# Attention with a gated feed-forward: the P.V sums and scores of the last two turns, and two output tiles

## The chip, the cores and the metric

The kernel runs on one core of a Trainium2 chip. The metric is the device time of one execution in microseconds; a kernel's time is the median over its runs. The engines are TensorE (PE, with its weight loads as PEld), VectorE (DVE), ScalarE (ACT), GpSimd (POOL) and SyncE (SP, which here only issues DMAs). Each works through its own instructions in program order and waits on semaphores of the others.

## The reference

With S = 2048 rows, D = 512, H = 32 heads of 16 and F = 1792:

```python
def _A_ref(x, wqkv, wo):
    qkv = ((x @ wqkv).reshape(B, S, 3, H, Dh)).transpose(2, 0, 3, 1, 4)
    q, k, v = qkv[0], qkv[1], qkv[2]
    scores = jnp.einsum("bhqd,bhkd->bhqk", q, k) * Dh ** -0.5
    o = jnp.einsum("bhqk,bhkd->bhqd", softmax(scores), v)
    return o.transpose(0, 2, 1, 3).reshape(B, S, D) @ wo

def _B_ref(x, w1, b1, w2, b2):
    h = jnp.einsum("bsd,df->bsf", x, w1) + b1
    r = jnp.where(h > 0, h, 0)
    return jnp.einsum("bsf,fd->bsd", r * r, w2) + b2

xn = _layernorm(A_x)
out = A_x + _A_ref(xn, A_wqkv, A_wo) * silu(_B_ref(xn, B_w1, B_b1, B_w2, B_b2))
```

## The kernel before

**Tiling.** After a first part (layer norm, transposes, queries, keys and values, written to DRAM) the attention runs in 512 steps `(qd, qc, kb)`: eight groups of four heads, four chunks of 512 queries, sixteen blocks of 128 keys. A step has two pairs of scores (`p` = 0, 1; two heads each, a tile of 128 keys x 2 x 512 queries), their exponentials in a tile `P`, and four matmuls of P.V (`values`, L572), each of which writes 32 of the 128 partitions of one PSUM bank: 16 value sums of a head and, from a column of ones, its row sum.

**Turns.** Eight steps make a turn, so there are 64 turns, and two of them make a chunk of queries for four heads. A turn `n` issues the 16 pairs of scores of the *next* eight steps and then the P.V matmuls of its own eight, 64 matmul records. The steps end at 511, so the last turn has 14 pairs. Between the scores TensorE does another product half by half (`lin`, L344, bank pair `spare`): the feed-forward, and in the last eight turns the projection with `wo`. The order within a turn is written out by hand as a string: `S` is a pair of scores into a tile "S", `0`, `1` and `B` are halves of a pair that go "aside", `L` is one step of the other product, `/` swaps the product's halves. Python code records the instructions in that order; no scheduler moves them (`manual_schedule`).

**PSUM.** The eight banks are: two rotating tiles "S" of two banks each (`BUFS["S"] = 2`), `spare` with two, and `sides[0]` ("acc") and `sides[1]` ("lin") with one each. `sides[0]` is also the bank in which P.V is summed. A pair in "S" is read by one exp of ScalarE straight out of PSUM (`exps`, L300, `P<-S`). An aside pair goes as two halves through `sides[0]` and `sides[1]`; VectorE copies each to the `P` tile (`aside`, L319), and ScalarE takes the exp in place (`P<-P`). Nine pairs are `direct` first, five (`pairs[9:14]`) are asides, and the last two are direct again but are held back in `later`: their exps are issued behind those of the asides. In the last turn those last two pairs don't exist.

**Sums.** `finish` copies the bank at the end of an even turn to `ou` (L583) and adds it to the bank at the end of the odd one (L586). The last turn leaves it to the end of the kernel (L880), where two adds of 128 x 256 do it.

**The end.** The last chunk of 512 rows needs the sums of the last turn. Behind its P.V stand: `ou` (L880), four matmuls with the identity that turn the row sums (L885), reciprocal, 16 matmuls that spread it (L892), the product (L904), a split in two parts (L905, L907), the projection (L704), the gate (L920), and the add of the input (L924, L927) or an accumulating store (L922). The third chunk's part of the same heads (`rest(i, dst)`, three matmuls of L704, and `end_rest(i, src)`) is spread among this: `rest(0)` stands in the last turn ahead of P.V and writes into a tile `two` of tag "S"; `rest(2)`, `rest(3)` and `rest(1)` come in the tail. `end_rest` gates a tile of 128 x 512 and adds it to the rows in DRAM with an accumulating DMA of POOL. Those rows were stored before from `base[2, i]`, which stays in SBUF.

Of the kernel before, what the change touches and what calls it, by code (L numbers as in the profile page):

```python
# [28 lines left out]
OP = mybir.AluOpType  # L29
# [45 lines left out]
def fast_path(tc, sb, ps, env):  # L75
# [4 lines left out]
    x, wqkv, wo, w1, b1, w2, b2, out = (  # L80
        env[n] for n in ("x", "wqkv", "wo", "w1", "b1", "w2", "b2", "out"))
    mm = nc.tensor.matmul
    dve, act, pool, sp = nc.vector, nc.scalar, nc.gpsimd, nc.sync
# [3 lines left out]
    def t(shape, dt, tag):  # L87

        cnt[0] += 1
        p = ps if tag in ("S", "lin", "acc") else sb  # L90
        if tag in BUFS:
            turn[tag] = turn.get(tag, -1) + 1
            n = turn[tag] % BUFS[tag]
            tag = f"{tag}{places[n] if tag == 'S' else n}"
        return p.tile(shape, dt, tag=tag, name=f"{tag}_{cnt[0]}")
# [194 lines left out]
    ptile = {}  # L290

    def score(i, p, hp, dst):
        qd, qc, kb = steps[i]
        k, q = ka[qd, kb // 8], qa[qd, qc]
        r = slice(64 * hp, 64 * hp + 64)
        mm(dst, k[r, p, 128 * (kb % 8):128 * (kb % 8) + 128], q[r, p], start=True, stop=True)  # L296

    def exps(i, p, src):
        if src is not None:
            act.activation(ptile[i, p], src, AF.Exp, scale=SCALE)  # L300

    def place(i, p):
        ptile[i, p] = t([128, 2, 512], FT, f"P{2 * ((i - 1) % 8) + p}")

    def scores(i, p):

        if i < len(steps):
            sc = t([128, 2, 512], FT, "S")
            place(i, p)
            for hp in range(2):  # L310
                score(i, p, hp, sc[:, hp])
            return sc

    def aside(i, p, hp):

        if hp == 0:
            place(i, p)
        score(i, p, hp, sides[hp])
        dve.tensor_copy(ptile[i, p][:, hp], sides[hp])  # L319

    gated, complete, gates = {}, set(), set()

# [35 lines left out]
    def lin(*halves):  # L358
        done = False
        if pair[0]:  # L360
            for half in halves:
                j = half ^ swapped[0]
                done |= pair[0][j].issue(half, lin_banks[j])
        return done

    def swap():
        if pair[0]:
            while lin(0, 1):
                pass
            f = pool.memset(note[:, notes[0]:notes[0] + 1], 0.0)  # L370
            notes[0] += 1
            for block in pair[0]:
                tc.add_manual_dep(f.ins, block.last, SYNC, reason="the products so far")
            swapped[0], fence[0] = 1, f.ins.name
# [53 lines left out]
    def second(c, g, i):  # L428
        ms = [m for m in range(len(PAIRS)) if PAIRS[m][0] == g]
        h, w = [hid[m] for m in ms], [wf[2, m] for m in ms]  # L430

        def evict():
            if g == 0:
                y[c, i] = t([128, 2, 512], FT, f"y{i}")
            old = b2b.unsqueeze(1).broadcast_to([128, 2, 512]) if g == 0 else y[c, i]
            dve.tensor_tensor(y[c, i], spare, old, op=OP.add)
            if g == 3:
                complete.add((c, i))

        return [Block(lambda p, k, j=j: h[k // 2][p][:, k % 2, 128 * j:128 * j + 128],  # L440
                      lambda p, k: w[k // 2][p][:, k % 2], range(2 * len(ms)), evict)
                for j in (2 * i, 2 * i + 1)]
# [8 lines left out]
    for c in ORDER:  # L451
        for m in range(len(PAIRS)):
            fill.append([lambda m=m: first(m)])
            if m in (1, 2, 4, 6):
                makes = [lambda c=c, g=m // 2, i=i: second(c, g, i) for i in range(2)]
# [113 lines left out]
    def values(i):  # L569
        qd, qc, kb = steps[i]  # L570
        for j in (1, 2, 3, 0) if i % 2 else (0, 1, 2, 3):
            mm(sides[0][32 * j:32 * j + 32], vq[qd][:, kb, 17 * j:17 * j + 32], ptile[i, j // 2][:, j % 2],  # L572
               start=kb % 8 == 0, stop=kb % 8 == 7)

    part = [None]

    def finish(n):

        if n == TURNS - 1:
            return  # L580
        ou = t([128, 512], FT, "ou")
        if n % 2 == 0:
            dve.tensor_copy(ou, sides[0])  # L583
            part[0] = ou
            return
        dve.tensor_tensor(ou, sides[0], part[0], op=OP.add)  # L586
        qd, qc, _ = steps[8 * n]
        sp.dma_start(zdram[qd][qc], ou[16::32])
        for j in range(4):
            sp.dma_start(udram[qd // 2][qc][0, qd % 2, :, j], ou[32 * j:32 * j + 16])  # L590
        events.setdefault(2 * n + 2, []).insert(0, (load_sums, (qd, qc)))
        events.setdefault(2 * n + 3, []).insert(0, (rowsums, (qd, qc)))
# [39 lines left out]
    wos, gsb, pend, onorm, base = [None], {}, {}, {}, {}  # L632
# [94 lines left out]
    TURNS, LAST = len(steps) // 8, 8 * (NQ - 1)  # L727
# [42 lines left out]
    def happen(time):  # L770
        for fn, a in events.pop(int(2 * time), ()):
            fn(*a)


    n = turn["S"]
# [5 lines left out]
    sides = [t([128, 512], FT, "acc"), t([128, 512], FT, "lin")]  # L781
# [6 lines left out]
    def end_rest(i, src):  # L788

        o = t([128, 512], FT, f"wf2{'hl'[i // 2]}{i % 2}")  # L790
        dve.scalar_tensor_tensor(o, src, 0.5, gsb[2, i // 2][:, i % 2], op0=OP.mult, op1=OP.mult)
        pool.dma_start(out[1024 + 128 * i:1152 + 128 * i], o, accum_op=OP.add)

    seen = t([1, 16], FT, "seen")

    def see(i):

        last = ptile[i, 1][:1, 1, 511:]
        act.copy(seen[:, :1], last)
        dve.tensor_tensor(seen[:, 8:9], last, sides[1][:1, :1], op=OP.max)  # L800
# [4 lines left out]
    ORDINARY = "SLLSBLLLSLL0SL1LSLL/SBLLSLL0SL1LSLL0L1SLS"  # L805
    TWO_PAIRS = "SLLLLBLLS/SL0LL1SLLSSEBLLLSLLLS/BLLSLL0LS1S"

    FIRST = "SLLSLLBLSLL0SL1LSLL/SBLLSLL0SL1LSLL0L1SLS"
    for n in range(TURNS):
        i = 8 * n  # L810
        happen(n)
        makes = fill[n][:]
        pair[0] = makes.pop(0)()
        if n:
            see(i - 1)
        pairs = [(k, p) for k in range(i + 1, i + 9) for p in range(2)]
        direct, asides = pairs[:9] + pairs[14:], pairs[9:14]
        later, aside_at = [], [0, 0]
        for row in TWO_PAIRS if makes else ORDINARY if n else FIRST:
            if row == "S":  # L820
                k, p = direct.pop(0)
                sc = scores(k, p)
                if k == i + 8:
                    later.append((k, p, sc))
                else:
                    exps(k, p, sc)
            elif row == "L":
                lin(0, 1)
            elif row in "01B":
                for hp in (0, 1) if row == "B" else (int(row),):  # L830
                    aside(*asides[aside_at[hp]], hp)
                    aside_at[hp] += 1
                if row != "B":
                    lin(1 - int(row))
            elif row == "/":
                swap()
                if n == TURNS - 1:
                    make_on((2, 3))
            else:
                end_pair()  # L840
                pair[0] = makes.pop(0)()
        for j, (k, p) in enumerate(asides):
            exps(k, p, ptile[k, p])
            if j == 0:
                for fn, a in middle.pop(n, ()):
                    fn(*a)
        for a in later:
            exps(*a)
        if n == TURNS - 1:
            two = t([128, 2, 512], FT, "S")  # L850
            rest(0, two[:, 0])
        pieces_now = pieces_of[n] if n < len(pieces_of) else 0
        ahead = pieces_now > 0 and n % per in (0, 1, 3, 6, 7, 10, 11)
        while lin(0, 1):
            pass
        if ahead:
            split_piece()
        end_pair()
        if n == LAST - 1:
            gsb.update({(2, i): y[2, i] for i in range(2)})  # L860
        if n == TURNS - 1:
            end_rest(0, two[:, 0])
        happen(n + 0.5)
        for _ in range(pieces_now - ahead):
            split_piece()
        for j in range(8):
            values(i + j)
        finish(n)
    for time in sorted(events):
        happen(time / 2)  # L870


    ou = t([128, 512], FT, "P0")
# [3 lines left out]
    h, l = t([128, 512], FR, "wf1h0"), t([128, 512], FR, "wf1l0")  # L877
    half = [slice(0, 256), slice(256, 512)]
    for s in half:
        dve.tensor_tensor(ou[:, s], sides[0][:, s], part[0][:, s], op=OP.add)  # L880
    small = t([128, 2, 512], FT, "S")
    lins = [small[:, 1], t([128, 512], FT, "lin"), t([128, 512], FT, "acc"), two[:, 0]]
    rest(2, spare[:, 0])
# [6 lines left out]
    for i in range(4):  # L890
        for j in range(4):
            mm(small[32 * j:32 * j + 32, 0, cut[i]], r[:, 4 * i + j:4 * i + j + 1].broadcast_to([128, 32]), ident,  # L892
               start=True, stop=True)
# [18 lines left out]
    o = [t([128, 512], FT, f"P{2 + i}") for i in range(4)]  # L912
    for j in range(2):
        for todo in ((0, 0), (0, 1)), ((1, 0),):
            for i in (2 * j, 2 * j + 1):
                group(lins[i], lambda p: (h, l)[p][:, cut[i]], lambda p: wlast[0][:, p],
                      start=len(todo) == 2, stop=len(todo) == 1, todo=todo)
        for i in (2 * j, 2 * j + 1):
            rows = out[1536 + 128 * i:1664 + 128 * i]
# [121 lines left out]
```

## Time and profile before

| | |
|---|---|
| median of 3 runs | 1227.74 us (1227.72 to 1228.27) |
| profiled execution | 1226.96 us, span 1224.9 us, granted clock 0.997 |
| TensorE busy | 1211.4 us (99%) |
| ScalarE busy | 1011.6 us (83%) |
| VectorE busy | 810.9 us (66%) |
| POOL busy | 279.6 us (23%) |

A timeline row has its start and length in us, the engine, the line, operation and operands, the count, and in brackets how long the engine stood idle before and what ended that. A chain row has start, length, engine, tile, line and count. A group has the count, then the busy time, the mean of one in ns, and the idle time ahead. A window has its length, the busy time and count of PE, PEld, DVE, ACT and POOL, the granted clock, the DMAs' share and GB/s. "P<-S" is an operation that reads a tile "S" and writes a tile "P"; numbers of buffers are left out.

### The profile page before, as it was taken

What the parts mean: (1) busy time and instruction counts of PE and PEld (TensorE: products, weight loads), DVE (VectorE), ACT (ScalarE), POOL (GpSimd) and SP (SyncE); (2) the same over time, 40 slices, a digit from 0 to 9 for tenths busy, and PEclk for the clock granted to TensorE, in tenths of its full rate; (3) what the DMA queues carried; (4) which work ended last, traced back from release to release, by engine and by line L of the source; (5) the groups of instructions that cost most, each with busy time, mean ns of one, the idle gap of its engine ahead of it and who ended that gap; (6) DMA issues with size and microseconds to landing.
All of it is one profiled execution on the core that took longest, in us unless ns stands there. A gap on an engine that the chain in (4) does not pass through costs nothing.

```text
span 1224.9 us, 24017 instructions
## 1 busy us (share of the span) xinstructions
PE 1211.4 (99%) x9925; PEld 717.4 (59%) x9925; DVE 810.9 (66%) x1293; ACT 1011.6 (83%) x1172; POOL 279.6 (23%) x223
## 2 busy tenths in 40 slices
PE   9999999999999999999999999999999999999997
PEld 8888755555555555555555555555555555555554
DVE  4542277676767775757686666676765758777776
ACT  4222489999999999999998998899999999999993
POOL 5000032122221220404022222130230403322212
PEclk9999999999999999999999999999999999999998
DMA  8675823232161323223423214141422232365445
GB/s 318 247 269 191 268 76 110 70 96 62 51 198 49 98 69 101 79 78 112 150 63 112 62 54 126 34 171 45 135 79 79 76 99 79 113 203 168 133 152 138
DMA packets 103750, 147.30 MB, mean 120 GB/s; under 512 B 42826, under 2 KB 57176, under 8 KB 102100
## 3 DMA queue, kind: packets, MB, share of 16 engines
q1 hardware_dynamic: 100484, 136.28, 35.0%
q0 software_dynamic: 2720, 8.65, 2.5%
q8 instruction: 79, 1.29, 0.4%
q10 hardware_dynamic: 432, 0.79, 0.2%
q14 instruction: 35, 0.29, 0.1%
HBM read 99.68 MB, written 46.00 MB: 119 GB/s over the span
## 4 chain that ended last, share of the span: by engine, by line
PE 97%; ACT 2%; DVE 0%; issue 0%; POOL 0%; DVEq 0%; POOLq 0%; ACTq 0%
PE acc L572 37%; PE spare L344 28%; PE S L296 14%; PE S L112 10%; PE acc L296 4%; ACT P L300 2%; PE lin L296 2%; PE lin L474 1%; PE S L210 1%; PE acc L112 0%; PE lin L112 0%; PE S L704 0%; PE acc L704 0%; DVE P L920 0%; DVE P L927 0%
## 5 line engine op out<-in xcount | busy, mean ns | idle before, releaser
L300 ACT ACTIVATE P<-S 128x1024 f32<-128x1024 f32 x704 | 664.5, 1037 | 91.3 <-PE S L296 91.3
L572 PE MATMUL acc<-P,V 128*32 128x512 f32 x4096 | 452.7, 594 | 0.0
L319 DVE COPY P<-acc 128x512 f32<-128x512 f32 x320 | 221.4, 692 | 143.6 <-PE lin L296 72.0
L300 ACT ACTIVATE P<-P 128x1024 f32<-128x1024 f32 x320 | 313.0, 1086 | 0.0
L572 PEld LDWEIGHTS acc<-P,V 128*32 128x32 f32 x4096 | 126.5, 110 | 287.4 <-issue 268.1
L296 PE MATMUL S<-QA,KA 64*128 64x512 f32 x1408 | 291.2, 403 | 3.0 <-ACT P L300 3.0
L319 DVE COPY P<-lin 128x512 f32<-128x512 f32 x320 | 219.4, 686 | 1.1
L296 PEld LDWEIGHTS S<-QA,KA 64*128 64x128 f32 x1408 | 134.1, 184 | 113.5 <-issue 43.5
L105 POOL TENSOR_TENSOR wf1l<-wr,wf1h 128x1024 fp32r<-128x1024 f32 x28 | 68.5, 2447 | 291.1 <-ACT wf1h L99 111.6
L296 PE MATMUL lin<-QA,KA 64*128 64x512 f32 x320 | 126.0, 394 | 0.0
L296 PE MATMUL acc<-QA,KA 64*128 64x512 f32 x320 | 125.8, 393 | 0.0
L370 POOL MEMSET note<- 1x1 f32 x68 | 6.1, 89 | 395.3 <-PE spare L344 392.9
L344 PE MATMUL spare<-xl,wf1h 64*128 64x512 f32 x464 | 96.1, 391 | 0.0
L105 POOL TENSOR_TENSOR hl<-T,hh 128x1024 fp32r<-128x1024 f32 x28 | 80.0, 2858 | 52.9 <-DVE hh L101 51.0
L344 PE MATMUL spare<-xh,wf1l 64*128 64x512 f32 x480 | 91.6, 390 | 0.0
L344 PE MATMUL spare<-wf2l,hh 64*128 64x512 f32 x448 | 91.0, 390 | 0.0
L105 POOL TENSOR_TENSOR wf2l<-wr,wf2h 128x1024 fp32r<-128x1024 f32 x28 | 67.2, 2399 | 90.3 <-DVE wf2h L101 90.3
L586 DVE TENSOR_TENSOR ou<-acc,ou 128x512 f32<-128x512 f32 x31 | 21.5, 692 | 97.6 <-PE acc L572 87.8
L344 PE MATMUL spare<-wf2h,hl 64*128 64x512 f32 x448 | 83.5, 390 | 0.0
L344 PE MATMUL spare<-xh,wf1h 64*128 64x512 f32 x480 | 77.1, 392 | 0.0
L344 PE MATMUL spare<-wf2h,hh 64*128 64x512 f32 x448 | 71.8, 392 | 0.0
L583 DVE COPY ou<-acc 128x512 f32<-128x512 f32 x32 | 22.2, 692 | 70.9 <-PE acc L572 70.5
(239 smaller groups left out, 1332.0 us busy)
## 6 DMA issues: line engine op xcount, KB each, us to landing
wr<-in_B_w_dram SPq DMA_DIRECT2D x56, 512.0 KB
KA<-kd SPq DMA_DIRECT2D x64, 256.0 KB
QA<-qd SPq DMA_DIRECT2D x128, 128.0 KB
kd<-P SPq DMA_DIRECT2D x15, 512.0 KB
qd<-P SPq DMA_DIRECT2D x15, 512.0 KB
u<-ud SPq DMA_DIRECT2D x15, 512.0 KB
V<-vd SPq DMA_DIRECT2D x8, 664.0 KB
vd<-P SPq DMA_DIRECT2D x16, 280.0 KB
```

Source lines behind the costliest of these rows:

```text
L105: leng.tensor_tensor(lo, src, hi.bitcast(FT), op=OP.subtract)
L112: mm(dst, lhs(a, k), rhs(b, k), start=n == 0, stop=n == len(todo) - 1)
L210: nc.tensor.transpose(pt[:, k, 128 * j:128 * j + 128], xnorm[c, i][:, j, 128 * k:128 * k + 128], ident)
L296: mm(dst, k[r, p, 128 * (kb % 8):128 * (kb % 8) + 128], q[r, p], start=True, stop=True)
L300: act.activation(ptile[i, p], src, AF.Exp, scale=SCALE)
L319: dve.tensor_copy(ptile[i, p][:, hp], sides[hp])
L344: ins = mm(bank, self.lhs(a, k)[r], self.rhs(b, k)[r], start=n == 0 and self.at[other] == 0, stop=n == len(self.todo[half]) - 1 and self.a ...
L370: f = pool.memset(note[:, notes[0]:notes[0] + 1], 0.0)
L474: mm(idle[:, :128], ident, ident, start=True, stop=True)
L572: mm(sides[0][32 * j:32 * j + 32], vq[qd][:, kb, 17 * j:17 * j + 32], ptile[i, j // 2][:, j % 2], start=kb % 8 == 0, stop=kb % 8 == 7)
L583: dve.tensor_copy(ou, sides[0])
L586: dve.tensor_tensor(ou, sides[0], part[0], op=OP.add)
```

## The change

In the last two turns P.V adds up in one bank without a copy between: the first matmul of turn 63 doesn't clear it, and `finish` does nothing for both turns. So `sides[0]` can't take scores in the last turn. That turn has its own string, `FINAL`, with eleven direct pairs and three asides, whose halves both go through `sides[1]`, one after the other. The last two direct pairs (`waits`) are held back behind the asides' exps, as the last two are in the other turns. At the end ScalarE copies the sums to `ou` in two halves where VectorE added them. `end_rest` for tiles 0 and 2 adds the kept `base` tile on POOL and stores with a plain DMA of SP; tiles 1 and 3 go on accumulating.

```diff
-    def aside(i, p, hp):
+    def aside(i, p, hp, bank):
...
-        score(i, p, hp, sides[hp])
-        dve.tensor_copy(ptile[i, p][:, hp], sides[hp])
+        score(i, p, hp, sides[bank])
+        dve.tensor_copy(ptile[i, p][:, hp], sides[bank])
...
             mm(sides[0][32 * j:32 * j + 32], vq[qd][:, kb, 17 * j:17 * j + 32], ptile[i, j // 2][:, j % 2],
-               start=kb % 8 == 0, stop=kb % 8 == 7)
+               start=kb % 8 == 0 and i // 8 < TURNS - 1, stop=kb % 8 == 7 and i // 8 != TURNS - 2)
...
-        if n == TURNS - 1:
+        if n > TURNS - 3:
             return
...
-        pool.dma_start(out[1024 + 128 * i:1152 + 128 * i], o, accum_op=OP.add)
+        rows = out[1024 + 128 * i:1152 + 128 * i]
+        if i % 2:
+            pool.dma_start(rows, o, accum_op=OP.add)
+        else:
+            pool.tensor_tensor(o, o, base[2, i // 2][:, 0], op=OP.add)
+            sp.dma_start(rows, o)
...
+    FINAL = "S0LSLLL1SLLS0LLSLL1S/LSLL0LSLLSL1LSLLLS"
...
         direct, asides = pairs[:9] + pairs[14:], pairs[9:14]
+        if n == TURNS - 1:
+            direct, asides = pairs[:9] + pairs[12:14], pairs[9:12]
+        waits = direct[-2:]
...
-        for row in TWO_PAIRS if makes else ORDINARY if n else FIRST:
+        for row in TWO_PAIRS if makes else FINAL if n == TURNS - 1 else ORDINARY if n else FIRST:
...
-                if k == i + 8:
+                if (k, p) in waits:
                     later.append((k, p, sc))
...
-                    aside(*asides[aside_at[hp]], hp)
+                    aside(*asides[aside_at[hp]], hp, 1 if n == TURNS - 1 else hp)
...
     for s in half:
-        dve.tensor_tensor(ou[:, s], sides[0][:, s], part[0][:, s], op=OP.add)
+        act.copy(ou[:, s], sides[0][:, s])
```

## The prediction

> **What bounds the kernel now.** I read the page first (engine shares, chain by engine), then the chain in order of time over the last 45 us, where every edit lies, then the timelines of TensorE and ScalarE there, and last the granted clock.
>
> ```profile
> PE 1211.4 (99%) x9925; PEld 717.4 (59%) x9925; DVE 810.9 (66%) x1293; ACT 1011.6 (83%) x1172; POOL 279.6 (23%) x223
> PE 97%; ACT 2%; DVE 0%; issue 0%; POOL 0%; DVEq 0%; POOLq 0%; ACTq 0%
> 1191.21 0.43 PE S L296 x2
> ...
> 1200.15 0.23 PE spare L344 x2
> 1200.38 0.91 PE S L704 x3
> 1201.29 7.00 PE acc L572 x64
> 1208.29 0.90 PE spare L704 x3
> 1209.19 0.79 PE lin L885 x8
> 1209.98 0.80 PE acc L704 x3
> ```
>
> TensorE carries 97% of the chain. In the last turn it runs without a hole: scores and projection from 1191.21, `rest(0)` (L704, three matmuls) at 1200.38, the P.V matmuls (L572) until 1208.29, then the tail. Any wait put ahead of `rest(0)` or of P.V goes straight into the time. ScalarE in the same turn, from the timeline and from the view of line L300:
>
> ```profile
> 1191.69 8.41 ACT L300 ACTIVATE P<-S 128x1024 f32<-128x1024 f32 x9 [1.52 <-PE S L296]
> 1199.96 4.86 ACT L300 ACTIVATE P<-P 128x1024 f32<-128x1024 f32 x5
> L300 ACT ACTIVATE P<-S x9: 1018/1029/1062, 1191.7 to 1199.0; 128x1024 f32<-128x1024 f32 x9
> L300 ACT ACTIVATE P<-P x5: 1072/1076/1086, 1200.0 to 1203.7; 128x1024 f32<-128x1024 f32 x5
> ```
>
> ScalarE has no gap from 1191.69 to 1204.82: nine exps out of PSUM, one every (8.41 - 1.03)/8 = 0.92 us, then five in place, one every (4.86 - 1.08)/4 = 0.945 us. It ends 4.4 us after TensorE has left the scores. That costs nothing now, because P.V takes the late tiles last: the last of its eight steps of 7.00/8 = 0.875 us begins at 1201.29 + 7 x 0.875 = 1207.4.
>
> **The change part by part.** *1. The last turn's scores.* Before, nine pairs of scores go through the two rotating buffers "S" and five through the banks "acc" and "lin"; after, eleven and three. TensorE's work is the same: in slots of 0.23 us (the row at 1200.15, one L of two matmuls) the old string has 9 S that are issued, 2 B, 6 digits and 21 L, the new one 11 S, 6 digits and 21 L: 38 each. Without a wait TensorE is again ready for `rest(0)` at 1200.4.
>
> The exps are as many too, 14, but their order matters. `waits` holds the tenth and eleventh direct pairs back behind the three in-place exps, so ScalarE runs nine direct, three in place, the tenth, the eleventh. The tile `two`, into which `rest(0)` writes, is the next "S" tile. Before, it is the tenth and takes the buffer of the eighth score, whose exp ends at 1191.69 + 7 x 0.92 + 1.03 = 1199.2, ahead of TensorE. After, it is the twelfth and takes the buffer of the tenth score, and that exp is the thirteenth in ScalarE's queue. It starts at 1199.96 + 3 x 0.945 = 1202.80 and ends at 1203.83. TensorE follows about 0.1 us later, as it does behind the fourth exp, which ends at 1191.69 + 3 x 0.92 + 1.03 = 1195.5:
>
> ```profile
> 1195.56 0.19 PEld L296 LDWEIGHTS S<-QA,KA 64*128 64x128 f32 x2 [0.17 <-ACT P L300]
> 1200.39 0.68 DVE L319 COPY P<-lin 128x512 f32<-128x512 f32 x1
> 1201.22 0.16 PEld L572 LDWEIGHTS acc<-P,V 128*32 128x32 f32 x8 [0.37 <-DVE P L319]
> ```
>
> So `rest(0)` starts at about 1203.9 instead of 1200.4: **+3.5 us**. Queued behind it on TensorE is all that is left: the 64 P.V matmuls, `rest(2)`, the sums, the last projection. ScalarE cannot be earlier: it has no idle time from 1191.69 on, and its first exp waits for a score behind the P.V of the turn before, which doesn't move. In the other turns the held-back exps are covered by the 7.00 us of P.V that stand between them and the next "S" tile; here nothing stands between. The eleven direct scores hold nothing else up: the eleventh needs the ninth exp, over at 1191.69 + 8.41 = 1200.10, and its slot is at about 1200.2. VectorE's copies are six instead of ten, so the in-place exps find their data. Bounds: a score that reaches ScalarE late adds its lateness. The third stands in the ninth slot, over at 1191.21 + 0.43 + 8 x 0.23 = 1193.5, just when ScalarE is free for it (1191.69 + 2 x 0.92): one slot, 0.23, at most. A pickup at once takes off 0.1, an exp that is 0.1 shorter as much. I keep 3.3 to 3.7.
>
> P.V no longer waits for the last copy out of the bank (loaded at 1201.22, copy over at 1201.07): 0 to -0.1, and I take 0. The DVE copy that ended turn 62 went on beside scores that didn't need it: 0.
>
> *2. The clock.* TensorE is now quiet from the end of the eleventh score, about 1200.6, to 1203.9: 3.3 us. What quiet does to the granted clock is seen at the two ends of the trace (TensorE's timeline, windows, groups of L474 in the windows 1 to 6.7 and 6.8 to 9 us):
>
> ```profile
> 1215.50 0.40 PE L704 MATMUL S<-QA,wf1l 128*128 128x512 f32 x1
> 1218.30:1218.40 0.10, 0.00 (x0) 0.00 (x0) 0.10 (x1) 0.00 (x0) 0.00 (x0) 1.00 1.00 184
> 1218.50:1218.60 0.10, 0.00 (x0) 0.00 (x0) 0.10 (x1) 0.00 (x0) 0.00 (x0) 0.50 1.38 225
> 1.39 6.36 PE L474 MATMUL lin<-ident 128*128 128x128 f32 x32 [1.39 <-POOL ident masks.py:199]
> L474 PE MATMUL lin<-ident 128*128 128x128 f32 x25 | 5.6, 422 | 1.4 <-POOL ident masks.py:199 1.4
> L474 PE MATMUL lin<-ident 128*128 128x128 f32 x15 | 2.1, 285 | 0.0
> ```
>
> The clock (third number from the right) falls from 1.00 to 0.50 at about 1218.45, 2.5 us after the last matmul ended at 1215.90. At the start the same matmul takes 422 ns until 6.7 us and 285 ns after, so work that began at 1.39 ran slowly for up to 5.3 us. A quiet of 3.3 us is longer than 2.5, so I expect the clock to fall in the hole, about 1203.1, or shortly after it, and to come back while P.V runs. At half clock each microsecond of P.V loses half of itself. The price lies between 0 (it doesn't fall) and 5.3/2 = 2.65. I take 1.5, a little over the middle: part of the slow stretch should lie in the hole itself.
>
> [...]
>
> *3. The sums and the tail.* Rows from the timeline, the groups and the DMA issues:
>
> ```profile
> 1208.44 0.76 DVE L880 TENSOR_TENSOR P<-acc,ou 128x256 f32<-128x256 f32 x2 [2.92 <-PE acc L572]
> L905 ACT CAST wf1h<-P 128x256 fp32r<-128x256 f32 x2 | 0.7, 404 | 7.6 <-DVE P L904 7.6
> 1209.23 0.69 DVE L791 SCALAR_TENSOR_TENSOR wf2l<-spare,y 128x512 f32<-128x512 f32 x1
> 1212.00 0.84 POOL L792 DMA_DIRECT2D out_dram<-wf2l  x1 [0.92 <-DVE wf2l L791]
> 1211.86 0.76 DVE L904 TENSOR_TENSOR P<-S,P 128x256 f32<-128x256 f32 x2 [0.15 <-PE spare L901]
> L683 POOL TENSOR_TENSOR hl<-T,hl 128x512 fp32r<-128x512 f32 x2 | 2.6, 1282 | 0.8 <-DVE hl L681 0.8
> L924 POOL TENSOR_TENSOR P<-P,KA 128x512 f32<-128x512 f32 x1 | 1.7, 1663 | 0.0
> 1203.99 0.40 SPq L649 DMA_DIRECT2D gl<-gd  x1
> wr<-in_A_x_dram POOLq DMA_DIRECT2D x3, 512.0 KB, 5.3
> 1214.30 0.69 DVE L920 SCALAR_TENSOR_TENSOR P<-S,gl 128x512 f32<-128x512 f32 x1
> ```
>
> Two ACT copies of 128x256 take about 0.7, as two casts of that size do, where VectorE took 0.76; both lie under `rest(2)` (1208.29 to 1209.19), behind which the row sums L885 stand on TensorE anyway. -0.1 to +0.1, taken as 0. If ScalarE were slow, L885 would show it at once.
>
> The add on POOL for tile 2 starts at 1209.23 + 0.69 + 0.1 = 1210.0 and takes 1.28 to 1.66, so POOL is free by 1211.7, before its next issue at 1212.00. On VectorE L904 has 0.15 us to spare; should the add slow VectorE's small steps beside it, up to 0.3 could come out. I take 0. On SP the store of tile 0 now stands ahead of the load of `gl`: its data are ready at 1203.9 + 0.9 + 0.7 + 1.7 = 1207.2, so the load leaves at about 1207.7 instead of 1203.99 and lands by 1213.0 with the 5.3 us of the slowest load of that size. L920 needs it at 1214.30 + 3.5 = 1217.8: 0, with 4.8 us of cover. The stores themselves land long before the last ones. 0.
>
> *Sum.* 3.5 + 1.5 = 5.0 us. The profiled execution took 1226.96 us (span 1224.9 and 2.1 around it), so 1232.0; the median of the runs is 0.8 above it: 1227.74 + 5.0 = **1232.7**.
>
> **The rivals.**
> *The clock holds* (0.30). [...] 1227.74 + 3.5 = 1231.2, between 1231.0 and 1231.5.
> *The clock stays low longer* (0.08): the hole counts against the stretch behind it too, as the first 5.3 us did: 3.5 + 2.65, 1233.9.
> *Half a hole* (0.08): ScalarE or the pickup is quicker than read here, so the wait shrinks to some 2 us, below the 2.5 at which the clock fell: 1229.7. That is within 0.2% (2.5 us), about what a measurement of this kernel can tell from no change.
> *Not slower* (0.04). `rest(0)` would be covered only if the thirteenth exp were over at 1200.4, which takes the hole below nothing; then the tail would decide, with P.V free of the copy (-0.1), ScalarE's sums (-0.1) and fewer accumulating stores: 1227.5. Against it stands ScalarE's gapless row of 14 exps. This is also what it would look like if the held-back order didn't take effect.
>
> **How the numbers follow.** The forecast, hole and clock, has 0.50. Low: 0.12 lies under 1230.6, where half a hole and no hole are left out. High: 1234.0 takes in the longer low clock. Range 1230.6 to 1234.0. Slower by over 0.2% (above 1230.2): 0.50 + 0.30 + 0.08 + a little of the half hole = 0.90; same 0.08; faster 0.02.
>
> **What would show it.** In the changed profile `rest(0)` (the first three L704 of "S" in the last turn) should start near 1203.9 with an idle of about 3.3 us that ACT P L300 ends, and the thirteenth exp should end just before. P.V should then take over 8 us instead of 7.00, with a granted clock below 1.00 in its window (the clock's rival: 7.00 and 1.00). L885 should follow `rest(2)` without a gap, POOL's next issue should not be late, and L930, the new number of L920, should not wait for `gl`. I am wrong if `rest(0)` starts within a microsecond of 1200.4, or if the tail behind P.V is shorter or longer by over 0.5 us.

## The result, and the profile after

The changed kernel takes 1233.22 us (1232.09 to 1234.17, six runs) against 1227.73 before: the ratio is 1.0044, 95% interval 1.0034 to 1.0053, so it is slower by 5.5 us. 1232.7 was forecast, with the wait of TensorE and the halved clock as its two terms.

The chain of the changed kernel in order of time, from the end of turn 62 on; the rows of the tail as far as they answer to those shown of before:

```profile
1192.39 0.45 PE S L296 x2
1192.84 0.02 issue
1192.86 9.02 ACT P L300 x10
1201.88 0.21 issue
1202.09 2.92 ACT P L300 x3
1205.01 0.04 issue
1205.06 1.36 PE S L704 x3
1206.42 8.21 PE acc L572 x64
1214.63 0.89 PE spare L704 x3
1215.52 0.80 PE lin L895 x8
...
1216.91 0.81 DVE ok L906
...
1218.59 0.43 DVE P L914
...
1224.77 0.68 DVE P L937
```

Where TensorE held the chain through the whole of turn 63, ScalarE now holds it for 13 exps, from the first one to the start of `rest(0)`. From the turn's first score to `rest(0)` it is 1205.06 - 1192.39 = 12.67 us, where it was 1200.38 - 1191.21 = 9.17: **+3.50**. The timeline shows the wait itself and the order of the exps:

```profile
1192.86 8.40 ACT L300 ACTIVATE P<-S 128x1024 f32<-128x1024 f32 x9 [1.54 <-PE S L296]
1201.14 2.95 ACT L300 ACTIVATE P<-P 128x1024 f32<-128x1024 f32 x3
1203.98 1.93 ACT L300 ACTIVATE P<-S 128x1024 f32<-128x1024 f32 x2
1201.43 0.39 PE L296 MATMUL S<-QA,KA 64*128 64x512 f32 x2
1205.06 0.51 PE L704 MATMUL S<-xh,hl 128*128 128x512 f32 x1 [3.24 <-ACT P L300]
```

The exps overlap without a gap (the nine end at 1201.26, the next begins at 1201.14), so the chain's 0.21 us of "issue" is no idle time. The eleventh score is through at 1201.82 (1201.43 + 0.39), the thirteenth exp (the first of the last two) starts at 1203.98, and TensorE stands for 3.24 us until it is over. The clock, from windows (the third number from the right is the granted clock):

```profile
1201.60:1205.10 3.50, 0.26 (x3) 0.05 (x1) 2.45 (x2) 3.50 (x5) 0.00 (x0) 1.00 0.01 5
1205.40:1205.50 0.10, 0.10 (x2) 0.10 (x1) 0.00 (x0) 0.10 (x1) 0.00 (x0) 0.55 0.91 348
1208.70:1208.80 0.10, 0.10 (x4) 0.00 (x0) 0.00 (x0) 0.00 (x0) 0.00 (x0) 0.50 0.00 0
1208.80:1208.90 0.10, 0.10 (x8) 0.03 (x4) 0.00 (x0) 0.00 (x0) 0.00 (x0) 0.89 0.00 0
```

It fell at about 1205.41, just after TensorE had begun again, and came back at about 1208.82: 3.4 us at half clock, all of it on work. `rest(0)` and P.V took 1214.63 - 1205.06 = 9.57 us instead of 1208.29 - 1200.38 = 7.91: **+1.66**. From the end of P.V to the end of VectorE's last add (1224.77 + 0.68 = 1225.45) it is 10.82 us, where it was 10.39 (1218.00 + 0.68 - 1208.29): **+0.43**. The last add in the kernel before:

```profile
1218.00 0.68 DVE P L927
```

These three make 5.6 us. The two profiled spans differ by 7.4, as 1.18 came before turn 63 and 0.63 behind the last add. Nearly all of the first lies in the opening: ScalarE waited for an input load there (next fence), which it didn't in the profile before, in code that the change doesn't touch. In the runs below turn 63 begins anywhere between 1191.4 and 1192.8. The second lies in the landing of the last stores, 5.9 to 7.9 us in the profiles below except that of e8_tail, which changes these stores.

```profile
10.26 0.62 ACT L161 CAST P<-KA 128x512 fp32r<-128x512 f32 x1 [1.15 <-DMA KA<-in_A_wqkv_dram]
```

### The profile page after: what moved, and what is told of

Its sections match the earlier page's. It is cut to its first block, busy times and chain, and to the rows that moved or that the text cites. A ratio compares the mean times of both kernels' runs of the same rounds, so it can differ in the third digit from the quotient of the medians.

```text
span 1232.3 us, 24016 instructions
## 1 busy us (share of the span) xinstructions
PE 1213.7 (98%) x9925; PEld 718.1 (58%) x9925; DVE 807.8 (66%) x1286; ACT 1011.3 (82%) x1174; POOL 280.1 (23%) x223
## 4 chain that ended last, share of the span: by engine, by line
PE 95%; ACT 3%; DMA 1%; DVE 0%; issue 0%; SPq 0%; DVEq 0%; ACTq 0%
PE acc L572 36%; PE spare L344 27%; PE S L296 14%; PE S L112 10%; PE acc L296 4%; ACT P L300 3%; PE lin L296 2%; DMA KA<-in_A_wqkv_dram 1%; PE S L210 0%; PE acc L112 0%; PE S L704 0%; PE lin L112 0%; DVE P L930 0%; DVE P L937 0%; SPq L132 0%
## 5 line engine op out<-in xcount | busy, mean ns | idle before, releaser
L319 DVE COPY P<-acc 128x512 f32<-128x512 f32 x315 | 217.9, 692 | 142.1 <-PE lin L296 77.2
```

The lines of the kernel that those rows point to most:

```text
L319: dve.tensor_copy(ptile[i, p][:, hp], sides[bank])
```

## The experiments

Each changes the changed kernel. The experiments e1 to e4 were timed on a chip where the kernel before took 1228.25 us (1227.13 to 1229.1), e5 to e8 on one where it took 1227.9 (1226.99 to 1228.85).

**The order of the exps** (e1_order).

```diff
-        waits = direct[-2:]
+        waits = direct[-2:] if n < TURNS - 1 else []
```

> The changed kernel, but the last turn's tenth and eleventh direct exps stay in their place in ScalarE's queue, ahead of the three in-place ones. My theory (TensorE waits because the buffer of `two` is read by the thirteenth exp of the queue): that exp is now the tenth, over at about 1192.9 + 9 x 0.92 + 1.03 = 1202.2 in the changed kernel's time, against TensorE ready at 1201.6, so the wait shrinks from 3.4 us to about 0.7, the clock stays at 1.00, P.V takes 7.0 us and the time is about 1228.6 (1228.0 to 1229.2). Rival (the time comes from eleven pairs through two buffers, or from halves that go one after the other through one bank): the wait stays over 2 us and the time over 1231.

1228.45 us, ratio to the kernel before 1.0003 (0.9993 to 1.0013). From its timelines, and a window over P.V:

```profile
1192.32 10.24 ACT L300 ACTIVATE P<-S 128x1024 f32<-128x1024 f32 x11 [1.53 <-PE S L296]
1202.42 2.97 ACT L300 ACTIVATE P<-P 128x1024 f32<-128x1024 f32 x3
1201.70 0.50 PE L704 MATMUL S<-xh,hl 128*128 128x512 f32 x1 [0.40 <-ACT P L300]
1202.60:1209.60 7.00, 7.00 (x65) 1.98 (x65) 3.04 (x4) 2.79 (x3) 1.29 (x1) 1.00 0.56 187
```

Eleven direct exps now run in one row, the wait is 0.40 us, and P.V takes 7.0 us at full clock. One line of order carries nearly all of the loss. Eleven pairs through two buffers and halves through one bank cost next to nothing.

**Another bank for `rest(0)`** (e2_bank). The order stays, the buffer changes.

```diff
-            rest(0, two[:, 0])
+            rest(0, sides[1])
...
-            end_rest(0, two[:, 0])
+            end_rest(0, sides[1])
```

> The changed kernel with the held-back order, but rest(0) writes into the bank sides[1], which the last aside's copy has left, instead of the next S tile. My theory: no wait ahead of rest(0) beyond 0.1 us, clock 1.00 through P.V, P.V 7.0 us, and about 1228.1 (1227.6 to 1228.7), where 0.4 over the kernel before is VectorE's slow step L906 in the tail. Rival (P.V itself needs the late exps): the wait moves into P.V and the time stays over 1230.

1228.75 us, 1.0004 (0.9995 to 1.0014), just above the 1227.6 to 1228.7 expected. The chain, and ScalarE's last two exps from the timeline:

```profile
1202.01 0.23 PE S L296 x2
1202.24 0.89 PE lin L704 x3
1203.13 7.00 PE acc L572 x64
1204.40 1.94 ACT L300 ACTIVATE P<-S 128x1024 f32<-128x1024 f32 x2
```

`rest(0)` follows the eleventh score without a gap and P.V takes 7.00, though ScalarE is as late as ever (its last two exps begin at 1204.40): it was `rest(0)` that waited, for its buffer, and not P.V. With e1 this shows the cause from both ends.

**Work in the hole** (e3_fill, e6_fill13, e7_fill6): `k` small matmuls, with k = 22, 13 and 6, before `rest(0)`.

```diff
+            for _ in range(k):
+                mm(sides[1][:, :128], ident, ident, start=True, stop=True)
             rest(0, two[:, 0])
```

> The changed kernel with 22 small matmuls on the identity (128x128 each, results not used) ahead of rest(0), about 3.1 us of TensorE work inside the wait. My theory (the slow P.V is the clock, which falls because TensorE is quiet): rest(0) starts when it did, 3.5 us later than in the kernel before, but the granted clock stays 1.00, rest(0) and P.V take 7.9 us instead of 9.6, and the time falls by 1.7 at most: about 1231.6 (1231.2 to 1232.2). Rival (P.V is slow because of what runs beside it, the exps and the transfers): P.V stays over 8 us, the time about 1233.2.

1232.97 us, 1.004 (1.0026 to 1.0054). I had reckoned 0.14 us for one; they took 0.235, ran 5.18 us and reached beyond the wait, so the time said nothing. The trace did: in the window over P.V it took 7.0 us at clock 1.00. The next two use fewer.

```profile
1206.70:1213.70 7.00, 7.00 (x66) 1.97 (x65) 2.14 (x3) 0.00 (x0) 1.28 (x1) 1.00 0.32 115
```

> The changed kernel with 13 small matmuls on the identity ahead of rest(0) (results not used), 13 x 0.235 = 3.1 us by the 22 of the run before, which took 5.18 us and so reached 1.7 us beyond the wait. My theory: they end before the thirteenth exp, rest(0) starts 3.5 us later than in the kernel before, the granted clock stays 1.00, rest(0) and P.V take 7.9 us, and the time is the kernel before plus 3.5 and 0.4 for the tail: about 1232.0 (1231.4 to 1232.4), with less spread from run to run than the changed kernel's 1232.1 to 1234.2. Rival (P.V is slow for another reason than the clock): P.V over 8 us, about 1233.5.

> The same with 6 of them: 1.4 us of work at the head of the wait, then some 2.0 us of quiet. It looks for the limit of the gate: no quiet between 0.7 us (e1_order, clock held) and 3.2 us (clock fell) has been seen in the main part. [...] If any quiet over about 1.5 us is enough, P.V takes over 8 us and the time is about 1233.5.

13 gave 1231.04 us (1.0027, 1.0016 to 1.0038), 6 gave 1231.65 (1.0031, 1.0019 to 1.0043). Chain (the turn's first score), timeline and window of the 13, then timeline and window of the 6, which leave 1.70 us of quiet; each matmul of the filler is two records:

```profile
1191.58 0.45 PE S L296 x2
1200.97 3.17 PE L862 MATMUL lin<-ident 128*128 128x128 f32 x26
1204.26 0.50 PE L704 MATMUL S<-xh,hl 128*128 128x512 f32 x1
1205.20:1212.20 7.00, 7.00 (x66) 1.97 (x65) 2.14 (x3) 0.00 (x0) 1.28 (x1) 1.00 0.39 135
```

```profile
1200.91 1.60 PE L862 MATMUL lin<-ident 128*128 128x128 f32 x12
1204.21 0.51 PE L704 MATMUL S<-xh,hl 128*128 128x512 f32 x1 [1.70 <-ACT P L300]
1205.10:1212.20 7.10, 7.10 (x66) 2.06 (x65) 2.15 (x3) 0.00 (x0) 1.28 (x1) 1.00 0.40 136
```

`rest(0)` starts as late as in the changed kernel (1204.26 is 12.7 us behind the turn's first score at 1191.58), the exps run as before, and useless work makes the kernel faster: it keeps the clock, and P.V takes 7.0 us. So the 1.66 us are the clock's. It is the traces that show this. The medians are 2.2 and 1.6 us below the changed kernel's, but were taken on another chip, and the intervals overlap with its 1.0034 to 1.0053. Both times came out below what I expected (13: 1231.4 to 1232.4; 6: about 1232.0, if the clock held), by less than the intervals.

In the profiled executions the clock fell for 3.24 us of quiet (3.23 in e4_acc below) and held for 1.70. For the other runs there is only the mean granted clock: 0.995 or 0.996 in each of the ten runs of the changed kernel and of e4_acc, 0.997 or 0.998 in the thirteen with 13 or 6 filler matmuls. It is a coarse sign, for the profiled run of e8_tail (below) reads 0.996 too, though it has `rest(0)` in the other bank, as e5_best, where nothing waits. The landing lowers the mean as well: in the kernel before the clock reads 0.50 from 1218.6 to the end of the span at 1224.9, and e8_tail has the longer landing.

**The tail** (e4_acc). Tile 2 goes back to the accumulating store.

```diff
-        if i % 2:
+        if i % 2 or i == 2:
```

> The changed kernel, but tile 2 goes back to the accumulating store of POOL (tile 0 keeps the add and the plain store). My theory for the tail: VectorE's L906 took 0.85 us instead of 0.27 because POOL's add ran beside it until its end; without the add it takes 0.27 again, from the end of P.V to the product L914 it is 3.57 us instead of 3.96, and the time is 0.4 below the changed kernel, which the times alone can't show. The wait ahead of rest(0) stays 3.4 us. Rival (the tail is longer because of ScalarE's copies): 3.96 stays.

1233.95 us, 1.0049 (1.0032 to 1.0066). I had expected 0.4 us below the changed kernel; it came out 0.7 above, within the spread of both, so only the trace can tell. VectorE and POOL in the tail, first of the kernel before (its L896 is the later L906) and of the changed kernel, then of e4_acc, with P.V and the clock's windows:

```profile
1210.54 0.27 DVE L896 TENSOR_SCALAR ok<-stat 128x32 f32<-128x32 f32 x1
1216.87 0.85 DVE L906 TENSOR_SCALAR ok<-stat 128x32 f32<-128x32 f32 x1
1218.59 0.75 DVE L914 TENSOR_TENSOR P<-S,P 128x256 f32<-128x256 f32 x2
1216.39 1.29 POOL L796 TENSOR_TENSOR wf2l<-wf2l,hl 128x512 f32<-128x512 f32 x1 [7.90 <-DVE wf2l L791]
```

```profile
1216.01 0.31 DVE L906 TENSOR_SCALAR ok<-stat 128x32 f32<-128x32 f32 x1
1217.39 0.76 DVE L914 TENSOR_TENSOR P<-S,P 128x256 f32<-128x256 f32 x2 [0.17 <-PE spare L911]
1213.77 0.89 PE spare L704 x3
1205.52 8.25 PE acc L572 x64
1204.50:1204.60 0.10, 0.10 (x2) 0.07 (x1) 0.00 (x0) 0.10 (x1) 0.00 (x0) 0.97 0.97 369
1208.00:1208.20 0.20, 0.20 (x8) 0.12 (x4) 0.00 (x0) 0.00 (x0) 0.00 (x0) 0.98 0.00 0
```

With the add on POOL, VectorE's step of 32 columns ends at 1217.72, 0.04 us after POOL's add (1217.68), and takes 0.85 us; without it, 0.31. All six traces that have the add (the changed kernel, e1, e2, e3, e6, e7) show this: 0.84 or 0.85 us, with an end 0.03 to 0.05 us after POOL's. From the end of P.V to L914 it is 3.96 us with the add (1218.59 - 1214.63) and 3.62 without (1217.39 - 1213.77). So 0.34 of the tail's 0.43 is this longer step. ScalarE's copies stayed, and the 3.62 are within 0.05 us of the 3.57 before (1211.86 - 1208.29). The clock fell at about 1204.59, 0.4 us after `rest(0)` had begun, came back at 1208.01, and P.V took 8.25 us: the hole and the clock don't depend on the tail.

**What is left of the change** (e5_best): e2_bank and e4_acc together.

> Both findings together: rest(0) into the bank sides[1] (as e2_bank) and tile 2 back to the accumulating store (as e4_acc); what is left of the change is P.V in one bank, three asides, ScalarE's copies and the add for tile 0. My theory: nothing of that lies on the chain, so L906 is 0.27 us, the tail is as in the kernel before, and the time is within 0.3 us of the kernel before. Rival (one of the other parts costs or gains on its own): over 0.5 us away from it, with the place seen in the trace.

1227.97 us, 0.9999 (0.999 to 1.0008). P.V in one bank, three asides, the copies on ScalarE and the add for tile 0 together neither gain nor cost more than the interval of about 1 us can tell: `rest(2)` follows P.V, L895 follows `rest(2)`:

```profile
1201.19 0.90 PE lin L704 x3
1202.08 7.00 PE acc L572 x64
1209.09 0.91 PE spare L704 x3
1209.99 0.79 PE lin L895 x8
```

**One add less on POOL** (e8_tail). On e5_best, tile 1 of the last chunk is stored with an accumulating DMA.

```diff
-            if i == 0:
+            if i < 2:
                 pool.dma_start(rows, o[i], accum_op=OP.add)
-            elif i == 1:
-                pool.tensor_tensor(o[i], o[i], base[3, j][:, i % 2], op=OP.add)
-                act.dma_start(rows, o[i])
```

> e5_best, and the add on POOL for the last chunk's tile 1 (L934) goes too: tile 1 is stored with an accumulating DMA as tile 0 is. If POOL's add slows VectorE's add beside it (L937 took 1.1 to 1.2 us for the first and 0.68 for the second), the first takes 0.68 too and VectorE ends 0.4 to 0.5 us earlier: 0.4 below e5_best, if the last stores then land earlier. Rival: the third accumulating store in a row lands last, and the end is as late as before or up to 1 us later.

1228.74 us, 1.0006 (0.9997 to 1.0015): 0.8 above e5_best, with runs that overlap (1228.03 to 1229.28 against 1226.9 to 1228.85). VectorE's last two adds, of e5_best and of e8_tail:

```profile
1217.76 1.81 DVE L937 TENSOR_TENSOR P<-P,KA 128x512 f32<-128x512 f32 x2
```

```profile
1217.40 1.28 DVE L934 TENSOR_TENSOR P<-P,KA 128x512 f32<-128x512 f32 x2
```

They take 1.28 us instead of 1.81 without POOL's add beside them, so the first half of the idea holds. But from their end to the end of the span it is 1227.5 - 1218.68 = 8.8 us, against 1226.1 - 1219.57 = 6.5. That fits the rival, that the landing of a third accumulating store took the gain and more. The size isn't settled by it, as the profiled execution of e8_tail is the slowest of its eleven (1229.28). No version beat the kernel before.

## Why the prediction was right

- *The wait for the thirteenth exp, +3.5 (3.3 to 3.7):* +3.50 measured. Each step can be read: ScalarE without a gap, thirteen exps, and `rest(0)` 0.05 us after the last of them (1205.01 to 1205.06). e1_order and e2_bank show the cause by taking away either the order or the buffer.
- *The clock, +1.5 out of 0 to 2.65:* +1.66 in the profiled execution, and the filler shows that it is the clock. That the size came so close is in part luck, as both guesses behind it were off and cancelled. I had allowed a slow stretch of up to 5.3 us, and it lasted 3.41 (1205.41 to 1208.82; 3.41 in e4_acc too). I had put part of it into the hole, and all of it lay on work: the clock fell not 2.5 us after the last score but 3.6, when TensorE had been busy again for 0.35. The 5.3 came from the longer matmuls of the opening, where the windows read a granted clock of 1.00 throughout, so no row shows that they were slow for the clock's sake.
- *The rival "the clock holds" (0.30):* out in the two traces with the whole hole, and by the mean clock, the coarse sign above, in the other eight runs.
- *The median, 1232.7 against 1233.22:* the times of the changed kernel stand in two groups, 1232.1 to 1232.4 and 1234.0 to 1234.2, and the median lies between them, where no run is. A slow stretch that in some runs begins inside the hole, and so costs less than 1.66 us, would make two groups, but no run shows one. The profiled execution (1234.05, the slow stretch wholly on work) is of the upper one; the lower one wasn't profiled, and the opening and the landing vary by as much, so this stays open.
- *The tail, taken as 0 with up to 0.3 for VectorE beside POOL's add:* +0.43, of which the add made 0.34. The term was mis-sized: I had named the slowing, but not that one small step would last to the very end of the add (0.85 us instead of 0.31). The 0.15 us that L904 had to spare couldn't take it.
- *ScalarE's copies, `gl`, POOL's queue, all 0:* as forecast for the time. The two copies took 0.65 us under `rest(2)`, L930 didn't wait, and e5_best is level with the kernel before. One of the signs failed: POOL's next issue was to be on time, and it came 4.36 us after the end of P.V (1218.99 - 1214.63) instead of 3.71 (1212.00 - 1208.29). POOL had long done its add by then and stood idle for 1.31 us until VectorE's gate (L791), which stands behind L906.

## What to carry to other kernels

Work that is put off in one engine's queue also puts off the release of the buffer it reads: here TensorE stood for 3.24 us. Before moving an instruction back, look for the next writer of that buffer and count what stands between the two: in 63 turns it was 7 us of P.V, in the last one nothing, and either an earlier place in the queue or another bank repaired it. A hole on TensorE can have a second price, the halved clock behind it: the one of 3.24 us had (1.66 us), the one of 1.70 us hadn't. And work for an engine that has idle time, as POOL had, isn't free when another engine's step on the critical path runs beside it: L906 took 0.85 us there instead of 0.31.

## What the runs showed of the hardware that was not expected

The clock held through 1.70 us of quiet in all six runs (mean 0.997 or 0.998) and fell for 3.24 us in all ten (0.995 or 0.996), as far as the mean clock tells, so for these two lengths nothing shows that it mattered where the hole lay. In the changed kernel's trace the clock fell at 1205.41, came back at 1208.82 and fell again at the end at about 1225.89 (it reads 0.95 from 1225.80 to 1225.90 and 0.50 after that). The time from the end of the last matmul ahead of the quiet to the fall was not the same each time: 3.59 us in turn 63 (from 1201.82, with TensorE busy again for the last 0.35), 3.27 at the end (from 1222.62), and 2.55 at the end of the kernel before (1215.90 to 1218.45). These three falls don't show what sets the moment. VectorE's 128x32 step beside POOL's add ended 0.04 us after the add (0.85 us instead of 0.31); it began 0.48 us into the add (1216.87 against 1216.39), and whether it stood until then or ran slowly isn't shown. And one more accumulating store of 256 KB among the last ones went with a landing some 2.3 us longer in the one profiled execution, and with 0.8 us more in the median, though VectorE ended 0.53 us earlier.
